# Pooled attention and a gated convolution block: a new order of the tokens in SBUF, 64x64 array tiles, and tanh as the mover

## The chip, the core and the metric

The kernel runs on one core of one Trainium2 chip. TensorE (PE in the profile) multiplies matrices into PSUM, ScalarE (ACT) applies functions element by element, VectorE (DVE) does elementwise arithmetic and copies, GpSimd (POOL) here mainly issues the loads, and SyncE (SP) issues the stores and the copies inside SBUF. Each engine works through its own list of instructions in order. The metric is the device time of one execution in microseconds; the less, the better.

## What is computed

Eight batches, eight heads, 576 tokens, 64 elements a head. Keys and values are averaged over groups of 8 tokens, so each head has 72 pooled keys; the attention output is the input `x` of a feed-forward block with a depthwise convolution over the tokens as its gate.

```python
k_p = k.reshape(B, H, Sp, pool, D).mean(axis=3)      # Sp = 576 / 8 = 72
v_p = v.reshape(B, H, Sp, pool, D).mean(axis=3)
scores = scale * np.matmul(q, k_p.transpose(0, 1, 3, 2))
attn = np.exp(scores - np.max(scores, axis=-1, keepdims=True))
attn = attn / (np.sum(attn, axis=-1, keepdims=True) + 1e-09)
x = np.matmul(attn, v_p)            # then heads side by side: (8, 576, 512)

h = np.maximum(x @ w_in, 0.0)       # (8, 576, 1024)
conv_out = sum over k of conv_w[k] * h shifted by k - 1 tokens
gate = 1.0 / (1.0 + np.exp(-conv_out))
return (h * gate @ w_out)           # (8, 576, 512), float32
```

The inputs are float32; on the chip everything but sums in PSUM and the output is bfloat16.

## The kernel before, in words

**Attention of a batch.** `k_tree` and `v_tree` add up groups of 8 tokens on DVE. `k_turn` transposes the pooled keys on PE and copies them to `kz`; `q_prep` does the same with the queries, 9 transposes at a time, to `qT`. In the queries' load each partition holds 36 neighbouring tokens of one head, and there are 16 such groups (`QG` = 16). So a score tile in PSUM has its columns in the order (two, i, g): token = g * 36 + 2 * i + two. `scores` runs two matmuls of 288 columns a head, and one exp on ACT (line 180) takes the 576 scores of 72 keys from PSUM and writes `attnT`, in the order of the tokens:

```python
out=at.rearrange("s (g i two) -> s two i g", two=2, g=QG),
```

The innermost index that is written is `g`, whose step in `attnT` is 36 elements, 72 bytes. `av` (lines 193 to 204) multiplies a stretch of 128 tokens of `attnT` with the pooled values of 8 heads, and DVE divides by the sums and writes `x`, token by token.

**From x to xT.** The block's first product needs `x` with the 512 features on the partitions. For batch 0, `xt` transposes on PE (20 small transposes) and copies on DVE. For all others `xt_dma` (line 216) does it by a transposing DMA from SBUF to SBUF, five a batch, issued on SP.

**The block.** `mm1(b, fb)` makes one of 8 blocks of 128 hidden features: 8 matmuls of 288 columns, and one relu on ACT into `hT`. `conv(b, g, c2)` works on 4 blocks and 288 tokens: the convolution is a matmul with diagonal weights `dw`, on 32x32 tiles of the array. There are 3 taps x 4 blocks x 4 row tiles = 48 matmuls (line 280), 16 tiles at work together, and for that block `j` puts its row tile `r` into column tile `(r + j) % 4`, so that all but the first block come out rotated by 32 j partitions. Two tanh on ACT (line 289) take them out of PSUM. Since the gate needs `h` in the same rotation, `mm1` issues two DMAs on SP (lines 264, 265) that copy the rotated block within SBUF, for six of 8 blocks, and `load_w_out` loads the rows of `w_out` rotated, in 7 DMAs. `gate` (lines 297, 299) is (tanh + 1) * h on DVE. `mm2` makes one tile of 128 tokens of the output, 8 matmuls of 512 columns, 9 tiles for a pair of batches, copied out by DVE and ACT in turn and stored by SP.

**The order.** It is written out by hand. `start` is batch 0's attention, `first_batch` is batch 0's block with batch 1's attention, and `batch(b)` puts eight `mm1(b)` in a row, with the second half of the convolution of batch b - 1, the steps `att[0]` to `att[6]` of the attention of batch b + 1, the first half of the convolution of b, and 4 or 5 output tiles of earlier batches between them. The keys are pooled and turned one batch earlier (`pool_keys(b + 2)` in the middle, `att[0]` at the end of `batch(b)`). The last batch has no attention beside it. All PSUM tiles come from one pool of four slots (`psum`, two banks each), used in turn, so an instruction on PE that needs a slot waits for the engine that reads the tile of four slots before. The loads of k, q and v have one buffer each; POOL issues the next one when the buffer has been read.

Of the kernel before, what the change touches and what calls it, by code (L numbers as in the profile page):

```python
# [16 lines left out]
def kernel(  # L17
# [10 lines left out]
    nc = tc.nc  # L28
# [7 lines left out]
    QR = S // QG  # L36
    NI = QR // 2
    SC = 288
    NS = S // SC
# [4 lines left out]
    KW = 3  # L44
    QD = 32
    NQ = P // QD
    n_grp = n_fb // NQ
    PAD = 2
    tok0 = [0, 128, 256, 384, S - P]
    row0 = [0, 0, 0, 0, P - S % P]  # L50

# [17 lines left out]
    def slot16(name):  # L69
        return psum.tile([P, 2, 2 * BANK], BF16, name=name, tag="slot")  # L70

    ident = const_pool.tile([P, P], BF16)
    ident32 = const_pool.tile([32, 32], FP32)
    seen = const_pool.tile([1, 1], BF16)
    w_in_sb = const_pool.tile([P, n_dmc, d_ff], BF16)
    w_out_sb = const_pool.tile([P, n_fb, d_model], BF16)
    cw_rows = const_pool.tile([KW * n_fb, P], FP32)
    convw = const_pool.tile([P, KW * n_fb], FP32)
    tile_id = const_pool.tile([P, QD], FP32)
    dw = const_pool.tile([P, KW, n_fb, QD], BF16)  # L80
    kz = [const_pool.tile([P, H, 2, Sp], BF16, name=f"kz{i}") for i in range(2)]
    va = [const_pool.tile([Sp, H, D + 1], BF16, name=f"va{i}") for i in range(2)]
    hT = [
        const_pool.tile([P, n_grp, 2 * NQ - 1, S + 2 * PAD], BF16, name=f"hT{i}") for i in range(2)
    ]

    def h_row(b, fb):
        g, j = divmod(fb, NQ)
        return hT[b % 2][:, g, j + NQ - 1 if j else 0, :]

# [78 lines left out]
    def scores(b, h):  # L169
        ps = slot("sc_ps")  # L170
        for c2 in range(2):
            nc.tensor.matmul(  # L172
                out=ps[0:Sp, c2, 0:SC],
                lhsT=kz[b % 2][:, h, c2, :],
                rhs=st[b]["qT"][:, h].rearrange("d i g -> d (i g)"),
                start=True,
                stop=True,
            )
        at = attnT_pool.tile([Sp, S], BF16, name="attnT")
        nc.scalar.activation(  # L180
            out=at.rearrange("s (g i two) -> s two i g", two=2, g=QG),
            in_=ps[0:Sp, :, 0:SC].rearrange("s two (i g) -> s two i g", g=QG),
            func=ACT.Exp,
            scale=1.0 / (POOL * 8.0),
        )
        st[b].setdefault("at", {})[h] = at
# [24 lines left out]

    def xt_dma(b, i):
        if "xT" not in st[b]:
            st[b]["xT"] = xT_pool.tile([P, n_pairs, S], BF16, name="xT")
        t0, r0 = i * P, row0[i]
        nc.sync.dma_start_transpose(
            out=st[b]["xT"][:, :, t0:t0 + P - r0],
            in_=st[b]["x"][i][r0:P].rearrange("p h d -> p (h d)"),
        )

    def xt(b, tiles):
        if "xT" not in st[b]:
            st[b]["xT"] = xT_pool.tile([P, n_pairs, S], BF16, name="xT")
        ps = slot16("xt_ps")
        w = sum(P - row0[i] for i in tiles)
        y = ps[:, 0, 0:n_pairs * w].rearrange("p (c n) -> p c n", c=n_pairs)
        t = 0
        for i in tiles:
            r0 = row0[i]
            n = P - r0  # L230
            for pr in range(n_pairs):
                nc.tensor.transpose(
                    out=y[:, pr, t:t + n],
                    in_=st[b]["x"][i][r0:P, 2 * pr:2 * pr + 2, :].rearrange("p h d -> p (h d)"),
                    identity=ident[r0:P, r0:P],
                )
            t += n
        t0 = tiles[0] * P
        nc.vector.tensor_copy(out=st[b]["xT"][:, :, t0:t0 + w], in_=y)

    def mm1(b, fb):
        xT = st[b]["xT"]
        ps = slot("h_ps")
        for c in range(NS):
            for dc in range(n_dmc):
                nc.tensor.matmul(  # L246
                    out=ps[:, c, 0:SC],
                    lhsT=w_in_sb[:, dc, fb * P:(fb + 1) * P],
                    rhs=xT[:, dc, c * SC:(c + 1) * SC],
                    start=(dc == 0),  # L250
                    stop=(dc == n_dmc - 1),
                )
        row = h_row(b, fb)
        nc.scalar.activation(  # L254
            out=row[:, PAD:S + PAD].rearrange("p (c n) -> p c n", c=NS),
            in_=ps[:, :, 0:SC],
            func=ACT.Relu,
            scale=0.5,
        )
        g, j = divmod(fb, NQ)  # L260
        if j:
            turned = hT[b % 2][:, g, j, :]
            cut = P - QD * j
            nc.sync.dma_start(out=turned[P - cut:P, PAD:S + PAD], in_=row[0:cut, PAD:S + PAD])
            nc.sync.dma_start(out=turned[0:P - cut, PAD:S + PAD], in_=row[cut:P, PAD:S + PAD])

    def conv(b, g, c2):
# [6 lines left out]
        for kk in range(KW):  # L274
            o0 = PAD - 1 + c2 * SC + kk
            for j in range(NQ):
                row = h_row(b, g * NQ + j)
                for r in range(NQ):
                    c = (r + j) % NQ
                    nc.tensor.matmul(  # L280
                        out=ps[j // 2][QD * c:QD * (c + 1), j % 2, 0:SC],
                        lhsT=dw[QD * r:QD * (r + 1), kk, g * NQ + j, :],
                        rhs=row[QD * r:QD * (r + 1), o0:o0 + SC],
                        start=(kk == 0),
                        stop=(kk == KW - 1),
                    )
        tg = tg_pool.tile([P, NQ, SC], BF16, name="tg")
        for i in range(2):
            nc.scalar.activation(  # L289
                out=tg[:, 2 * i:2 * i + 2, :], in_=ps[i][:, :, 0:SC], func=ACT.Tanh  # L290
            )
        st[b]["tg", g, c2] = tg

    def gate(b, g, c2):
# [6 lines left out]
            in0=t1,  # L301
            in1=hT[b % 2][:, g, 0:NQ, PAD + c2 * SC:PAD + (c2 + 1) * SC],
            op=OP.mult,
# [27 lines left out]

    def load_w_out(j):
        src = moe_w_out.rearrange("(g j p) m -> j p g m", j=NQ, p=P)
        dst = w_out_sb.rearrange("p (g j) m -> j p g m", j=NQ)
        cut = P - QD * j
        nc.gpsimd.dma_start(out=dst[j, P - cut:P], in_=src[j, 0:cut])
        if j:
            nc.gpsimd.dma_start(out=dst[j, 0:P - cut], in_=src[j, cut:P])

    def build_conv_w():  # L340
# [4 lines left out]
        nc.vector.tensor_copy(out=convw, in_=ps[:, 0, 0:KW * n_fb])  # L345
        for r in range(NQ):
            nc.vector.tensor_copy(
                out=tile_id[QD * r:QD * (r + 1), :],
                in_=ident[QD * r:QD * (r + 1), QD * r:QD * (r + 1)],
            )  # L350
        nc.vector.tensor_tensor(
            out=dw.rearrange("p k f j -> p (k f) j"),
            in0=tile_id.unsqueeze(1).to_broadcast([P, KW * n_fb, QD]),
            in1=convw.unsqueeze(2).to_broadcast([P, KW * n_fb, QD]),
            op=OP.mult,
        )

    HH = H // 2

    def start():  # L360
# [7 lines left out]
        for i in range(2):  # L368
            nc.vector.memset(kz[i], 0.0)
            nc.vector.memset(va[i][:, :, D], float(POOL))  # L370
            nc.gpsimd.memset(hT[i][:, :, :, 0:PAD], 0.0)
            nc.gpsimd.memset(hT[i][:, :, :, S + PAD:S + 2 * PAD], 0.0)
        landed(st[0]["k"][0:1, 0, 0, 0:1])
# [16 lines left out]
        landed(st[1]["q"][0:1, 0, 0:1])  # L390
        for j in range(NQ):
            load_w_out(j)
        build_conv_w()
        k_tree(0, 0, HH)
        k_turn(0, 0, HH)
# [17 lines left out]
    def attention(n):  # L413
# [24 lines left out]
        def a5():  # L438
            for i in range(3):
                av(n, i)  # L440
                xt_dma(n, i)

        def a6():
            for i in range(3, 5):
                av(n, i)
                xt_dma(n, i)

        return [a0, a1, a2, a3, a4, a5, a6]

# [8 lines left out]
    def first_batch():  # L458
# [24 lines left out]
        gate(0, 1, 1)  # L483
        pool_keys(2)
        st[2]["att"] = attention(2)
        st[2]["att"][0]()

    def batch(b):
        none = lambda: None
        att = st[b + 1]["att"] if b + 1 < B else [none] * 7  # L490
        tiles = list(range(4)) if b % 2 else list(range(4, 9))

        def tile_out():
            if tiles:
                mm2(b - 1, tiles.pop(0))

        mm1(b, order[0])
        if b > 1:
            conv(b - 1, 1, 0)
        att[1]()  # L500
        if b > 1:
# [3 lines left out]
        if b > 1:  # L505
            conv(b - 1, 1, 1)
        att[2]()
        if b > 1:
# [3 lines left out]
        tile_out()  # L512
        att[3]()

        mm1(b, order[3])
        tile_out()
        att[4]()

        mm1(b, order[4])
        conv(b, 0, 0)  # L520
        att[5]()
        gate(b, 0, 0)
        if b + 2 < B:
            pool_keys(b + 2)
            st[b + 2]["att"] = attention(b + 2)

        mm1(b, order[5])
        conv(b, 0, 1)
        att[6]()
        gate(b, 0, 1)  # L530
# [3 lines left out]
        if len(tiles) > 1:  # L534
            tile_out()

        mm1(b, order[7])
        if b + 2 < B:
            st[b + 2]["att"][0]()
        tile_out()  # L540
# [41 lines left out]
```

## Time and profile before

| what | value |
|---|---|
| median of 3 runs | 363.75 us (363.26 to 364.43) |
| the profiled execution's own time | 364.43 us |
| its span on the core | 362.7 us |
| PE busy | 244.8 us, 67% |
| ACT busy | 244.9 us, 68% |
| DVE busy | 145.7 us, 40% |
| mean granted PE clock | 0.849 |
| read from HBM, written | 32.52 MB, 9.44 MB |

The profile is one execution. "Busy" is time in which an engine had an instruction under way; matmuls overlap each other, so the rate of a stream of matmuls is read from the starts of the groups in the timeline and not from the duration of one. The chain of waits follows the work that ended last back to its cause. A batch in the middle of the run takes 41 us from the first `mm1` of one to that of the next.

### The profile page before, as it was taken

What the parts mean: (1) busy time and instruction counts of PE and PEld (TensorE: products, weight loads), DVE (VectorE), ACT (ScalarE), POOL (GpSimd) and SP (SyncE); (2) the same over time, 40 slices, a digit from 0 to 9 for tenths busy, and PEclk for the clock granted to TensorE, in tenths of its full rate; (3) what the DMA queues carried; (4) which work ended last, traced back from release to release, by engine and by line L of the source; (5) the groups of instructions that cost most, each with busy time, mean ns of one, the idle gap of its engine ahead of it and who ended that gap; (6) DMA issues with size and microseconds to landing.
All of it is one profiled execution on the core that took longest, in us unless ns stands there. A gap on an engine that the chain in (4) does not pass through costs nothing.

```text
span 362.7 us, 7083 instructions
## 1 busy us (share of the span) xinstructions
PE 244.8 (67%) x3013; PEld 148.2 (41%) x3013; DVE 145.7 (40%) x265; ACT 244.9 (68%) x209; POOL 30.3 (8%) x58
## 2 busy tenths in 40 slices
PE   0533874338669486499666966589745985699995
PEld 0413642226235253265334643255423652365642
DVE  5512670095008350084502941075601960072341
ACT  1596289914994179943997369962999389945531
POOL 5525110001000010000100010000100000000000
PEclk9999995557858878969987898969996898579999
DMA  6997994038604954049911986139731531035323
GB/s 110 144 145 118 152 178 75 2 66 143 131 29 73 167 109 101 29 71 198 164 48 57 111 173 125 43 62 187 146 85 41 88 109 47 29 76 153 116 78 145
DMA packets 47155, 37.38 MB, mean 103 GB/s; under 512 B 23036, under 2 KB 41492, under 8 KB 47124
## 3 DMA queue, kind: packets, MB, share of 16 engines
q0 software_dynamic: 16976, 16.27, 30.0%
q1 hardware_dynamic: 30148, 20.67, 23.5%
q8 instruction: 23, 0.38, 0.4%
q14 instruction: 8, 0.07, 0.1%
HBM read 32.52 MB, written 9.44 MB: 116 GB/s over the span
## 4 chain that ended last, share of the span: by engine, by line
ACT 41%; PE 26%; DVE 12%; issue 10%; DMA 9%; POOL 0%; DVEq 0%; SPq 0%; ACTq 0%; POOLq 0%
ACT attnT L180 35%; PE h_ps L246 11%; PE o_ps L312 7%; DMA xT<-x 7%; DVE x L204 3%; PE c_ps L280 3%; PE q_ps L159 3%; ACT tg L289 2%; DMA qr<-in_q_dram 2%; DVE gT L299 2%; PE av_ps L193 2%; ACT hT_107 L254 1%; DVE r L203 1%; ACT hT_108 L254 1%; DVE kdup L135 1%
## 5 line engine op out<-in xcount | busy, mean ns | idle before, releaser
L180 ACT ACTIVATE attnT<-sc_ps 72x576 bf16<-72x576 f32 x64 | 163.2, 2883 | 11.1 <-PE sc_ps L172 11.1
L246 PE MATMUL h_ps<-xT,w_in_sb 128*128 128x288 bf16 x512 | 91.8, 334 | 9.7 <-DMA xT<-x 8.3
L312 PE MATMUL o_ps<-w_out_sb,gT 128*128 128x512 bf16 x288 | 71.0, 396 | 12.4 <-ACT attnT L180 11.5
L246 PEld LDWEIGHTS <-w_in_sb 128*128 128x128 bf16 x512 | 56.0, 112 | 36.3 <-DMA xT<-x 9.5
L203 DVE RECIPROCAL r<-av_ps 128x8 f32<-128x8 f32 x40 | 8.0, 200 | 133.6 <-PE av_ps L193 133.6
L254 ACT ACTIVATE hT_108<-h_ps 128x576 bf16<-128x576 f32 x32 | 23.9, 746 | 42.1 <-PE h_ps L246 42.1
L312 PEld LDWEIGHTS <-gT 128*128 128x128 bf16 x288 | 29.0, 101 | 46.6 <-issue 18.5
L254 ACT ACTIVATE hT_107<-h_ps 128x576 bf16<-128x576 f32 x32 | 24.5, 767 | 33.8 <-PE h_ps L246 33.8
L289 ACT ACTIVATE tg<-c_ps 128x576 bf16<-128x576 f32 x64 | 38.5, 661 | 2.8 <-PE c_ps L280 2.8
L193 PEld LDWEIGHTS <-attnT 72*128 72x128 bf16 x320 | 18.2, 123 | 27.1 <-issue 16.5
L172 PE MATMUL sc_ps<-qT,kz_104 128*72 128x288 bf16 x64 | 14.2, 321 | 22.1 <-ACT attnT L180 21.7
L172 PE MATMUL sc_ps<-qT,kz_103 128*72 128x288 bf16 x64 | 14.4, 341 | 20.6 <-ACT attnT L180 19.4
L204 DVE TENSOR_TENSOR x<-av_ps,r 128x512 bf16<-128x512 f32 x40 | 27.7, 692 | 1.4
L280 PEld LDWEIGHTS <-dw 32*32 32x32 bf16 x1536 | 15.8, 91 | 24.5 <-issue 18.2
L320 ACT COPY o<-o_ps 128x512 f32<-128x512 f32 x16 | 9.4, 589 | 22.4 <-PE o_ps L312 22.4
L322 DVE COPY o<-o_ps 128x512 f32<-128x512 f32 x20 | 13.8, 690 | 25.5 <-PE o_ps L312 25.5
L164 DVE COPY qT<-q_ps 128x1152 bf16<-128x1152 bf16 x16 | 12.1, 758 | 25.6 <-PE q_ps L159 25.4
L193 PE MATMUL av_ps<-va_105,attnT 72*128 72x65 bf16 x160 | 10.5, 232 | 13.7 <-ACT attnT L180 13.5
L172 PEld LDWEIGHTS <-kz_104 128*72 128x72 bf16 x64 | 7.4, 121 | 28.9 <-issue 27.2
L172 PEld LDWEIGHTS <-kz_103 128*72 128x72 bf16 x64 | 8.3, 132 | 26.8 <-issue 22.8
L99 POOL DMA_DIRECT2D kr<-in_k_dram x9 | 7.3, 814 | 136.8 <-DVE t_840 L121 27.2
L280 PE MATMUL c_ps<-hT_107,dw 32*32 32x288 bf16 x768 | 14.3, 340 | 6.2 <-ACT attnT L180 3.8
(162 smaller groups left out, 176.7 us busy)
## 6 DMA issues: line engine op xcount, KB each, us to landing
out_dram<-o SPq DMA_DIRECT2D x36, 256.0 KB, 2.3
qr<-in_q_dram POOLq DMA_DIRECT2D x8, 576.0 KB, 6.1
kr<-in_k_dram POOLq DMA_DIRECT2D x7, 576.0 KB, 8.4
vr<-in_v_dram POOLq DMA_DIRECT2D x7, 576.0 KB, 8.1
hT_107<-hT_107 SPq DMA_DIRECT2D x16, 108.0 KB, 2.2
hT_108<-hT_108 SPq DMA_DIRECT2D x16, 108.0 KB, 2.9
hT_107<-hT_107 SPq DMA_DIRECT2D x16, 72.0 KB, 5.1
hT_108<-hT_108 SPq DMA_DIRECT2D x16, 72.0 KB, 4.5
```

Source lines behind the costliest of these rows:

```text
L164: nc.vector.tensor_copy(out=st[b]["qT"][:, :, i0:i0 + n, :].rearrange("d h i g -> d i h g"), in_=ps[:, 0:n * P].rearrange("d (i h g) -> d ...
L172: nc.tensor.matmul(out=ps[0:Sp, c2, 0:SC], lhsT=kz[b % 2][:, h, c2, :], rhs=st[b]["qT"][:, h].rearrange("d i g -> d (i g)"), start=True, s ...
L180: nc.scalar.activation(out=at.rearrange("s (g i two) -> s two i g", two=2, g=QG), in_=ps[0:Sp, :, 0:SC].rearrange("s two (i g) -> s two i ...
L193: nc.tensor.matmul(out=ps[:, h // 4, c:c + D + 1], lhsT=st[b]["at"][h][:, t0:t0 + P], rhs=va[b % 2][:, h, :], start=True, stop=True,)
L203: nc.vector.reciprocal(out=r, in_=y[:, :, :, D])
L204: nc.vector.tensor_tensor(out=x.rearrange("p (g h) d -> p g h d", g=2), in0=y[:, :, :, 0:D], in1=r.unsqueeze(3).to_broadcast([P, 2, 4, D]) ...
L246: nc.tensor.matmul(out=ps[:, c, 0:SC], lhsT=w_in_sb[:, dc, fb * P:(fb + 1) * P], rhs=xT[:, dc, c * SC:(c + 1) * SC], start=(dc == 0), stop ...
L254: nc.scalar.activation(out=row[:, PAD:S + PAD].rearrange("p (c n) -> p c n", c=NS), in_=ps[:, :, 0:SC], func=ACT.Relu, scale=0.5,)
L280: nc.tensor.matmul(out=ps[j // 2][QD * c:QD * (c + 1), j % 2, 0:SC], lhsT=dw[QD * r:QD * (r + 1), kk, g * NQ + j, :], rhs=row[QD * r:QD * ...
L289: nc.scalar.activation(out=tg[:, 2 * i:2 * i + 2, :], in_=ps[i][:, :, 0:SC], func=ACT.Tanh)
L312: nc.tensor.matmul(out=ps[:, 0, :], lhsT=gT[:, fb, j * P:(j + 1) * P], rhs=w_out_sb[:, fb, :], start=(fb == 0), stop=(fb == n_fb - 1),)
L322: nc.vector.tensor_copy(out=o, in_=ps[:, 0, :])
```

## The change

- exp writes `attnT` in the order (i, two, g): 16 neighbouring elements, then the next 16. The tokens in `attnT`, and in `x`, now stand in the order (i, two, g).
- `xt` serves all batches, `xt_dma` goes. Its transposes take a permutation matrix `perm` (built once by `build_perm`) in place of the identity, write PSUM in runs of 8 elements, and the DVE copy writes `xT` in the order of the tokens, in runs of 16 elements.
- The convolution uses 64x64 tiles: 24 matmuls on 4 tiles. Every second block comes out with its two halves swapped. The tanh of those blocks is split in two of 64 partitions, each of which writes the other half's partitions; so `tg` is in the natural order.
- `hT` has no rotated copies, and their DMAs are gone; `w_out` is loaded in two DMAs.
- The attention has nine steps in place of seven: `a7` and `a8` are the transposes. All nine run within one batch: `att[0]` after the first `mm1`, and so on; `att[7]` ahead of the last `mm1`, `att[8]` after it, ahead of the last output tile.

```diff
     hT = [
-        const_pool.tile([P, n_grp, 2 * NQ - 1, S + 2 * PAD], BF16, name=f"hT{i}") for i in range(2)
+        const_pool.tile([P, n_fb, S + 2 * PAD], BF16, name=f"hT{i}") for i in range(2)
     ]
...
         nc.scalar.activation(
-            out=at.rearrange("s (g i two) -> s two i g", two=2, g=QG),
+            out=at.rearrange("s (i two g) -> s two i g", two=2, g=QG),
             in_=ps[0:Sp, :, 0:SC].rearrange("s two (i g) -> s two i g", g=QG),
...
-    def xt_dma(b, i):
...
     def xt(b, tiles):
...
-        w = sum(P - row0[i] for i in tiles)
-        y = ps[:, 0, 0:n_pairs * w].rearrange("p (c n) -> p c n", c=n_pairs)
...
+        w = len(tiles) * RT
+        y = ps[:, 0, 0:n_pairs * QG * w].rearrange("p (c g r) -> p c g r", c=n_pairs, g=QG)
+        for ii, i in enumerate(tiles):
             for pr in range(n_pairs):
                 nc.tensor.transpose(
-                    out=y[:, pr, t:t + n],
-                    in_=st[b]["x"][i][r0:P, 2 * pr:2 * pr + 2, :].rearrange("p h d -> p (h d)"),
-                    identity=ident[r0:P, r0:P],
+                    out=y[:, pr, :, ii * RT:(ii + 1) * RT],
+                    in_=st[b]["x"][i][:, 2 * pr:2 * pr + 2, :].rearrange("p h d -> p (h d)"),
+                    identity=perm,
                 )
...
+        nc.vector.tensor_copy(
+            out=st[b]["xT"].rearrange("p c (g r) -> p c g r", g=QG)[:, :, :, r0:r0 + w - skip],
+            in_=y[:, :, :, skip:w],
+        )
...
-        g, j = divmod(fb, NQ)
-        if j:
-            turned = hT[b % 2][:, g, j, :]
-            cut = P - QD * j
-            nc.sync.dma_start(out=turned[P - cut:P, PAD:S + PAD], in_=row[0:cut, PAD:S + PAD])
-            nc.sync.dma_start(out=turned[0:P - cut, PAD:S + PAD], in_=row[cut:P, PAD:S + PAD])
...
-            for j in range(NQ):
-                row = h_row(b, g * NQ + j)
-                for r in range(NQ):
-                    c = (r + j) % NQ
...
+            for p2 in range(2):
+                for j in range(2):
+                    fb = g * NQ + 2 * p2 + j
+                    for r in range(2):
+                        c = (r + j) % 2
+                        nc.tensor.matmul(
+                            out=ps[j][HP * c:HP * (c + 1), p2, 0:SC],
+                            lhsT=dw[HP * r:HP * (r + 1), kk, fb, :],
+                            rhs=hT[b % 2][HP * r:HP * (r + 1), fb, o0:o0 + SC],
+                            start=(kk == 0),
+                            stop=(kk == KW - 1),
+                        )
         tg = tg_pool.tile([P, NQ, SC], BF16, name="tg")
-        for i in range(2):
+        pairs = tg.rearrange("p (p2 j) n -> p p2 j n", j=2)
+        nc.scalar.activation(out=pairs[:, :, 0, :], in_=ps[0][:, :, 0:SC], func=ACT.Tanh)
+        for c in range(2):
+            r = 1 - c
             nc.scalar.activation(
-                out=tg[:, 2 * i:2 * i + 2, :], in_=ps[i][:, :, 0:SC], func=ACT.Tanh
+                out=pairs[HP * r:HP * (r + 1), :, 1, :],
+                in_=ps[1][HP * c:HP * (c + 1), :, 0:SC],
+                func=ACT.Tanh,
             )
...
-            out=dw.rearrange("p k f j -> p (k f) j"),
-            in0=tile_id.unsqueeze(1).to_broadcast([P, KW * n_fb, QD]),
...
+            in0=tile_id.unsqueeze(1).to_broadcast([P, KW * n_fb, HP]),
...
+    def build_perm():
+        nc.vector.tensor_copy(
+            out=perm.rearrange("p (g r) -> p r g", r=RT),
+            in_=ident.rearrange("p (r g) -> p r g", r=RT),
         )
...
-        for j in range(NQ):
-            load_w_out(j)
+        for i in range(2):
+            load_w_out(i)
         build_conv_w()
+        build_perm()
...
     def attention(n):
...
+        def a7():
+            xt(n, [0, 1])
+
+        def a8():
+            xt(n, [2, 3])
+            xt(n, [4])
...
         mm1(b, order[4])
         conv(b, 0, 0)
-        att[5]()
+        att[4]()
+        pool_keys(b + 2)
         gate(b, 0, 0)
-        if b + 2 < B:
-            pool_keys(b + 2)
-            st[b + 2]["att"] = attention(b + 2)

         mm1(b, order[5])
         conv(b, 0, 1)
-        att[6]()
+        att[5]()
         gate(b, 0, 1)

         mm1(b, order[6])
         tile_out()
         if len(tiles) > 1:
             tile_out()
-
+        att[6]()
+
+        att[7]()
         mm1(b, order[7])
-        if b + 2 < B:
-            st[b + 2]["att"][0]()
+        att[8]()
         tile_out()
```

## The prediction, written before the changed kernel ran

> **What bounds the kernel now.** First the page's chain of work and its costliest groups: the engine that is longest on the chain has one line that stands out.
>
> ```profile
> ACT 41%; PE 26%; DVE 12%; issue 10%; DMA 9%; POOL 0%; DVEq 0%; SPq 0%; ACTq 0%; POOLq 0%
> L180 ACT ACTIVATE attnT<-sc_ps 72x576 bf16<-72x576 f32 x64 | 163.2, 2883 | 11.1 <-PE sc_ps L172 11.1
> L289 ACT ACTIVATE tg<-c_ps 128x576 bf16<-128x576 f32 x64 | 38.5, 661 | 2.8 <-PE c_ps L280 2.8
> ```
>
> Exp and tanh read the same 576 float32 from PSUM and write 576 bfloat16, yet one exp is 2.88 us and one tanh 0.66. They differ in the function and in the place of the written elements (72 bytes apart against side by side). Second, the rates, from ACT's timeline, of instructions that follow each other:
>
> ```profile
> 13.13 20.06 ACT L180 ACTIVATE attnT<-sc_ps 72x576 bf16<-72x576 f32 x8 [11.11 <-PE sc_ps L172]
> 348.50 2.28 ACT L289 ACTIVATE tg<-c_ps 128x576 bf16<-128x576 f32 x4
> ```
>
> 2.51 us for each exp, 0.57 for each tanh. Third, who waits for it:
>
> ```profile
> PE sc_ps L172 <- ACT attnT L180: 41.1, 30, 2.1
> PE av_ps L193 <- ACT attnT L180: 22.2, 12, 2.2
> PE o_ps L312 <- ACT attnT L180: 11.5, 9, 1.5
> PE h_ps L246 <- DMA xT<-x: 8.3, 4, 4.7
> PE c_ps L280 <- ACT attnT L180: 7.4, 6, 1.6
> ```
>
> PE stands 82 us for exp (slots of `psum`, or `attnT` itself) and 8 for the transposing DMA. Last, the stages (length, PE, PEld, DVE, ACT, POOL busy, granted clock, DMA share, GB/s): start, batch 0, a middle batch, the last batch, the tail.
>
> ```profile
> 0.00:39.06 39.06, 13.06 (x103) 9.54 (x104) 16.86 (x41) 21.34 (x9) 16.70 (x40) 1.00 0.91 134
> 39.06:82.66 43.60, 23.61 (x356) 16.31 (x356) 19.36 (x34) 29.38 (x24) 3.26 (x4) 0.69 0.49 87
> 211.10:252.60 41.50, 30.07 (x378) 18.14 (x379) 17.78 (x31) 30.39 (x26) 2.22 (x3) 0.88 0.57 105
> 329.88:347.80 17.92, 17.92 (x290) 10.70 (x289) 6.96 (x11) 10.19 (x17) 0.00 (x0) 1.00 0.45 146
> 347.80:362.70 14.90, 10.37 (x137) 4.68 (x136) 4.39 (x7) 4.03 (x7) 0.00 (x0) 1.00 0.29 107
> ```
>
> The last batch, which has no attention beside it, takes 17.9 us with PE never idle at full clock; the same block with attention takes 41.5. So the middle batches are set by exp, and below it lies a PE bound that these rows allow to be added up.
>
> **The parts of the change.**
>
> *Exp in runs of 16.* Bounds: 0.57 us each, as tanh, or 2.51, as now. Nearest is DVE's `qT` copy, whose output too stands in runs of 16 (1152 elements in 0.76 us, 0.66 ns each; the plain `xT` copy takes 0.68 for 1024, the same rate): runs of 16 cost nothing there. I take 0.6. The Trainium skill (SBUF — State Buffer, the note on cachelines) says an engine needs at least two hits in a 16-byte line for full bandwidth; this run has eight, the present order one. ACT in a middle batch: 8 exp at 0.6, 8 relu at 0.65, 4 x 3 tanh at 0.57, 2.25 copies at 0.58: 18.1 us in place of 30.4. The third tanh costs 32 x 0.57 = 18 us of ACT in all, hidden under PE while ACT's sum is below PE's; only the tail's last pair shows.
>
> *Transposes on PE.* Seven batches x 20. The row is `q_prep`, 9 in 0.50 us where they follow each other:
>
> ```profile
> 288.48 0.50 PE q_ps L159 x9
> ```
>
> So 20 x 0.056 = 1.1 us a batch. The new output has steps in PSUM, which no row shows for PE: at worst the 0.31 us of a lone transpose in the groups (`xt_ps`, 309 ns), 6.2 us a batch; no gain is possible. I take 1.1, the nearest in kind and density. The Trainium skill (TensorE: Matmul & The Clock Gate, on PE-mode transposes) speaks against moving them: it gives about 275 ns each inside a kernel. By that figure it would be 5.5 us a batch and the forecast some 30 us later; the row says 56 ns. DVE gains three copies (0.68, 0.68, 0.28) a batch, 17.8 to 19.4 us: still under PE. The wait for the DMA (5 to 8 us on the chain at each batch's first `mm1`) goes; late next is the copy of tile 4, under the last output tile's 1.73 us.
>
> *The convolution.* Now 48 matmuls in 0.67 us, three rounds of 16 tiles; then six rounds of four. A round can't be shorter than a stream of 288 columns (`mm1`: eight in 0.98, 0.122 each): 0.73. As long as now's rounds (0.22): 1.34. So +0.06 to +0.67 a call; I take +0.2, nearer the stream, since a round has four weights to load and not 16. 32 calls: 6 us (2 to 21).
>
> *Copies of h.* 96 DMA issues leave SP's queue, 35 transposes too; SP keeps 36 stores. The chain has 1.9 us of waiting for these copies at one place: no more is counted. `w_out`: two DMAs for seven on POOL, same bytes; its wait for landings sets the time, not the issue: nothing. `perm` and a `dw` twice as wide put about 1.2 us (0.96 again, and a copy of 0.25) ahead of `k_tree(0)` on DVE; q lands at 9.45, after the turned keys (8.9): 0.3 us shows.
>
> *PE's sum for a middle batch.* 17.92 (8 `mm1`, 4 conv, 4 output tiles) + 0.87 (half a tile, the mean is 4.5) + scores 16 x 0.122 = 2.0 + `q_prep` 1.0 + `k_turn` 0.3 + `av` 40 x 0.055 = 2.2 (16 took 0.78 to 0.87 at the densest) + 1.1 transposes + 0.8 conv = 26.2. Above ACT (18.1) and DVE (19.4), so PE is the bound. Not all will be packed: each convolution wants two of four slots, which three tanh (1.7 us) hold longer than two did, and at step `att[4]` ACT gets tanh x 3, exp x 2, relu, tanh x 3 in a row, some 5.5 us against PE's 3; following the slots by hand there, PE waits 0.8 to 1.5 us. With DVE's order (`pool_keys`, 2.6 us, now ahead of `gate` and the `x` of `av`) I allow 2.2 a batch: 28.4, against 41.2 (247.2 us from 82.66 to 329.88, six batches).
>
> *The start.* Eight exp at 0.6 save 15.3 us; `av` then waits for v_tree, whose v lands at 15.7 and which is through by 18.5; `mm1` 5.8 us later as now: 24.5. `w_in` is complete at 23.6. So 14.5 off. *Batch 0*: v of batch 1 is issued at 29.74 and takes 8.1 us: 37.8, behind landings which the change doesn't move. Then on DVE: v_tree 2.3, gates 3 x 1.2, five `x` at 0.88, three copies 1.7: 49.8. I take 51 for batch 1's first `mm1` (82.66 now).
>
> *Sum.* 51 + 6 x 28.4 + last batch 17.9 + 0.8 + tail 14.9 + 1.0 (a tanh, two conv) = 256 us of span. Outside it 364.43 - 362.70 = 1.7, and the profiled run is 0.7 above the median: **257 us**.
>
> **Rivals.** (a) *Exp stays as slow*: its time is in the function, or 16-element runs don't help. For: no ACT row has such runs. Against: the `qT` copy. ACT's batch is then 8 x 2.51 + 5.2 + 6.8 + 1.3 = 33.4, and of its 11 idle us some 6 stay: 39.4; start 38.5, batch 0 43: 38.5 + 43 + 6 x 39.4 + 18.7 + 15.9 + 1 = about 353. (b) *A PE part is dear*: transposes at 0.31 (+5 a batch, 7 batches: 292), or the four tiles take turns (24 x 0.122 = 2.93 a call, +2.26 x 32: with the 6 taken out, 323). Against: 16 tiles work together now at 0.22 a round. (c) *The loads become the bound*: the queues' shares, 30.0% and 23.5% of 362.7, are 194 us of 16 engines, 24 a batch with the copies that go; under 28.4, so it is hidden; it decides from 28.4 up, and a tenth above that, 31 a batch, is 273. (d) *Slower*: PE's clock. It drops to 0.5 after idle stretches (0.69 in batch 0, where one `mm1` took 2.08 in place of 0.98). If a packed PE were held at half, a batch would be 52 us and the whole over 450; it decides from a clock of 26.2 / 41.2 = 0.64 down. Against: the last batch ran at 1.00.
>
> **How the numbers follow.** My case 80% (242 to 283: conv at +0.06 and stalls of 0.5 a batch give 242, conv at +0.67 and stalls of 4 give 283; its own range, 245 to 272, is between); (b) and (c), or an exp between the ends, 13% (272 to 323); (a) 4%; (d) 3%. The range 243 to 288 takes in nearly all of the first and the cheaper part of (b) and (c), and leaves out (a), (d) and the dear ends of (b). 0.3% is about what a measurement here can tell from no change: faster 0.96, same 0.01, slower 0.03.
>
> **What would show it.** Right: exp near 0.6 us a piece; no PE wait for `attnT` above a us; the middle batches at 27 to 30 us with PE over 90% busy and the clock near 1; conv at 0.73 to 1.0 a call; `mm1` starting at 24 to 26 us. Wrong: exp above 1.2; `xt_ps` at 0.2 us a piece in its stream; PE waiting for tanh or for slots over 4 us a batch; the first `mm1` of a batch waiting for DVE's `xT`.

## The result, and the profile after

The changed kernel takes 258.87 us (median of 4 runs, 257.91 to 259.77) against 363.5 us for the one before beside it (361.25 to 364.43): a ratio of 0.713, 95% interval 0.709 to 0.717. The forecast was 257, with a range of 243 to 288. The profiled execution has a span of 257.0 us.

The same views in the same order as before. First the page: the chain by engine, the exp group and the group of the two half tanh.

```profile
PE 57%; ACT 20%; DVE 12%; DMA 6%; issue 3%; POOL 0%; POOLq 0%
L176 ACT ACTIVATE attnT<-sc_ps 72x576 bf16<-72x576 f32 x64 | 37.0, 646 | 18.5 <-PE sc_ps L168 18.3
L273 ACT ACTIVATE tg<-c_ps 64x576 bf16<-64x576 f32 x64 | 41.3, 645 | 1.2
```

Exp was 2883 ns a piece and is 646, the same as the half tanh (645); the 163.2 us of the group became 37.0. PE now leads the chain. ACT's timeline gives the pace of instructions that follow each other (start, length, count):

```profile
124.39 0.65 ACT L270 ACTIVATE tg<-c_ps 128x576 bf16<-128x576 f32 x1
125.06 1.30 ACT L273 ACTIVATE tg<-c_ps 64x576 bf16<-64x576 f32 x2
126.39 1.18 ACT L176 ACTIVATE attnT<-sc_ps 72x576 bf16<-72x576 f32 x2
```

0.59 us for each exp (0.6 was assumed, 2.51 before) and 0.65 for each half tanh. Third, from the list of what PE waits for, the rows that the argument needs: us in total, times, the longest.

```profile
PE kT_ps L143 <- DVE kdup L131: 5.1, 3, 4.3
PE xt_ps L216 <- DVE x L200: 3.1, 6, 0.9
PE h_ps L233 <- DVE xT L223: 2.5, 2, 2.2
PE c_ps L261 <- ACT attnT L176: 2.2, 6, 0.4
PE c_ps L261 <- ACT tg L273: 1.1, 6, 0.2
```

The 82 us of waiting for exp are now 2.2 us. Last the stages (length, then PE, PEld, DVE, ACT, POOL busy, granted clock, DMA share, GB/s): start, batch 0, batch 1, a middle batch with four output tiles and one with five, the last batch, the tail.

```profile
0.00:24.86 24.86, 11.61 (x103) 8.70 (x104) 17.72 (x40) 5.80 (x9) 10.54 (x30) 0.92 0.90 128
24.86:52.91 28.05, 21.09 (x262) 14.97 (x262) 17.43 (x32) 16.98 (x28) 6.34 (x9) 0.93 1.00 152
52.91:81.01 28.10, 26.28 (x246) 17.60 (x246) 18.87 (x32) 13.75 (x23) 3.04 (x4) 0.90 0.65 114
...
109.72:137.03 27.31, 26.00 (x295) 17.58 (x294) 19.47 (x34) 17.63 (x29) 2.22 (x3) 1.00 0.54 104
137.03:165.75 28.72, 27.64 (x304) 18.38 (x303) 18.87 (x33) 18.81 (x31) 2.22 (x3) 1.00 0.54 109
...
221.93:240.89 18.96, 18.74 (x197) 11.50 (x198) 6.77 (x11) 13.34 (x21) 0.00 (x0) 1.00 0.13 50
240.89:257.00 16.11, 10.57 (x89) 5.03 (x88) 4.42 (x7) 5.64 (x9) 0.00 (x0) 0.98 0.28 106
```

In a middle batch PE is busy for 95 or 96% of the time at clock 1.00, where it was 72% at 0.88. Of the 105.7 us that went from the span, 14.2 went in the start (39.06 to 24.86), 15.6 in batch 0 (43.6 to 28.05), 78 in the six batches (247.2 to 169.0); the last batch and the tail gave back 1.0 and 1.2.

### The profile page after: what moved, and what is told of

It is laid out like the page before. It is cut to its first block, busy times and chain, and to the rows that moved or that the text cites. A ratio compares the mean times of both kernels' runs of the same rounds, so it can differ in the third digit from the quotient of the medians.

```text
span 257.0 us, 5560 instructions
## 1 busy us (share of the span) xinstructions
PE 223.3 (87%) x2385; PEld 148.2 (58%) x2385; DVE 158.2 (62%) x285; ACT 147.2 (57%) x241; POOL 28.0 (11%) x53
## 4 chain that ended last, share of the span: by engine, by line
PE 57%; ACT 20%; DVE 12%; DMA 6%; issue 3%; POOL 0%; POOLq 0%
PE o_ps L298 24%; PE h_ps L233 18%; ACT attnT L176 6%; PE c_ps L261 6%; DMA qr<-in_q_dram 6%; ACT tg L273 5%; PE q_ps L155 4%; DVE x L200 4%; ACT tg L270 3%; DVE o L308 3%; ACT hT_108 L240 3%; ACT hT_109 L240 2%; PE xt_ps L216 2%; PE sc_ps L168 1%; PE av_ps L189 1%
## 5 line engine op out<-in xcount | busy, mean ns | idle before, releaser
L233 PE MATMUL h_ps<-xT,w_in_sb 128*128 128x288 bf16 x512 | 75.7, 294 | 5.9 <-DVE xT L223 2.5
L176 ACT ACTIVATE attnT<-sc_ps 72x576 bf16<-72x576 f32 x64 | 37.0, 646 | 18.5 <-PE sc_ps L168 18.3
L273 ACT ACTIVATE tg<-c_ps 64x576 bf16<-64x576 f32 x64 | 41.3, 645 | 1.2
L240 ACT ACTIVATE hT_109<-h_ps 128x576 bf16<-128x576 f32 x32 | 20.8, 651 | 33.2 <-PE h_ps L233 32.9
L240 ACT ACTIVATE hT_108<-h_ps 128x576 bf16<-128x576 f32 x32 | 20.9, 652 | 19.6 <-PE h_ps L233 19.3
L261 PEld LDWEIGHTS <-dw 64*64 64x64 bf16 x768 | 22.1, 105 | 13.9 <-issue 12.0
L306 ACT COPY o<-o_ps 128x512 f32<-128x512 f32 x16 | 9.4, 586 | 28.2 <-PE o_ps L298 28.2
L270 ACT ACTIVATE tg<-c_ps 128x576 bf16<-128x576 f32 x32 | 20.8, 650 | 3.4 <-PE c_ps L261 3.3
L261 PE MATMUL c_ps<-hT_108,dw 64*64 64x288 bf16 x384 | 16.7, 287 | 2.6 <-ACT attnT L176 1.1
L216 PE MATMUL xt_ps<-perm,x 128*128 128x128 bf16 x160 | 14.0, 227 | 4.8 <-DVE x L200 3.1
L261 PE MATMUL c_ps<-hT_109,dw 64*64 64x288 bf16 x384 | 16.4, 286 | 1.6 <-ACT attnT L176 1.1
L216 PEld LDWEIGHTS <-x 128*128 128x128 bf16 x160 | 10.8, 100 | 7.2 <-DVE x L200 5.9
L155 PE MATMUL q_ps<-ident,qr 128*128 128x128 bf16 x144 | 12.0, 237 | 1.9 <-DMA qr<-in_q_dram 1.9
```

What stands on the lines that cost most here:

```text
L155: nc.tensor.transpose(out=ps[:, i * P:(i + 1) * P], in_=st[b]["q"][:, i0 + i, :], identity=ident)
L176: nc.scalar.activation(out=at.rearrange("s (i two g) -> s two i g", two=2, g=QG), in_=ps[0:Sp, :, 0:SC].rearrange("s two (i g) -> s two i ...
L216: nc.tensor.transpose(out=y[:, pr, :, ii * RT:(ii + 1) * RT], in_=st[b]["x"][i][:, 2 * pr:2 * pr + 2, :].rearrange("p h d -> p (h d)"), id ...
L233: nc.tensor.matmul(out=ps[:, c, 0:SC], lhsT=w_in_sb[:, dc, fb * P:(fb + 1) * P], rhs=xT[:, dc, c * SC:(c + 1) * SC], start=(dc == 0), stop ...
L240: nc.scalar.activation(out=hT[b % 2][:, fb, PAD:S + PAD].rearrange("p (c n) -> p c n", c=NS), in_=ps[:, :, 0:SC], func=ACT.Relu, scale=0.5,)
L261: nc.tensor.matmul(out=ps[j][HP * c:HP * (c + 1), p2, 0:SC], lhsT=dw[HP * r:HP * (r + 1), kk, fb, :], rhs=hT[b % 2][HP * r:HP * (r + 1), f ...
```

## The experiments

Theory: exp's write, 72 bytes from element to element, was the bound; with it gone PE is, and the other parts are judged by what they add to PE or make it wait for. The main rival: the gain comes from the DMAs that the change removes.

### Exp alone, in the kernel before

```diff
-            out=at.rearrange("s (g i two) -> s two i g", two=2, g=QG),
+            out=at.rearrange("s (i two g) -> s two i g", two=2, g=QG),
```

> The kernel before with one line changed: exp writes (i, two, g). Nothing puts the tokens back in order, so the convolution sees other neighbours and the output is not the reference's; every instruction and transfer is otherwise the one of before. Theory (the whole gain is exp's write, and the other parts of the change are its price): ACT's batch falls to 30.4 - 8 x 1.92 = 15 us, PE's sum is 17.92 + 0.87 + 2.0 + 1.0 + 0.3 + 2.2 = 24.3 a batch, plus 1 to 3 us of waiting for the transposing DMA: 26.5 a batch, 24.9 + 28 + 6 x 26.5 + 17.9 + 14.9 + 1.7 = about 246, between 240 and 262. Rival (the DMAs that the change removed would have become the bound): the first mm1 of each batch waits 5 us and more for xT, 31 a batch, 270 to 285.

Measured: 266.31 us (263.81 to 268.89), ratio 0.729 (0.720 to 0.737). The one line brings 27.1% of the time, of 28.7% for the whole change. It landed between the two sums, closer to the rival's 270. PE's waits and one batch of this kernel show why.

```profile
PE h_ps L246 <- DMA xT<-x: 15.7, 6, 4.7
PE kT_ps L147 <- DVE kdup L135: 12.2, 3, 8.3
```

```profile
120.71:149.92 29.21, 25.27 (x368) 16.18 (x371) 17.00 (x30) 15.12 (x26) 2.21 (x3) 0.94 0.82 158
```

PE's 25.3 us is 1.0 above the sum of 24.3. The DMA wait is 2.6 us at each of six places, as allowed. The sum missed two things. Batch 1's first `mm1` starts at 57.95 us and not at 52.9, behind one wait of 8.3 us for the keys of batch 2; the kernel before has 6.0 us of this wait at the same place. And a middle batch takes 28.5 us in the mean, not 26.5: beside the wait itself, in this batch the matmuls behind it run at half the pace for a while (eight of `mm1` in 2.05 us, where they take 1.07 otherwise), at a mean clock of 0.94. So exp is the cause of the gain, and the transposing DMA is late once the batch is short.

### The old exp in the changed kernel

```diff
-            out=at.rearrange("s (i two g) -> s two i g", two=2, g=QG),
+            out=at.rearrange("s (g i two) -> s two i g", two=2, g=QG),
```

> The changed kernel with exp writing in steps of 72 bytes again, as before; the tokens then stand in another order than the permutation expects, so the output is not the reference's, with the same instructions. Theory (exp's write is the cause): exp is back at 2.5 us, ACT bounds the middle batches at 33.4 + 6 = 39 us, about 353. Rival (the gain came from the DMAs that went): 260 to 300.

Measured: 386.08 us (385.33 to 386.91), ratio 1.060 (1.051 to 1.068): slower than the kernel before, though 131 fewer DMAs are issued inside SBUF (96 copies of h, 35 transposes). The rival falls. The price of 353 was wrong too. Two middle batches and PE's waits:

```profile
171.30:214.50 43.20, 32.03 (x292) 20.35 (x294) 19.46 (x34) 33.06 (x29) 2.22 (x3) 0.80 0.34 66
214.50:259.72 45.22, 34.81 (x300) 21.52 (x302) 18.86 (x33) 34.26 (x31) 2.23 (x3) 0.77 0.34 69
```

```profile
PE sc_ps L168 <- ACT attnT L176: 36.5, 26, 2.1
PE c_ps L261 <- ACT attnT L176: 26.0, 18, 2.2
```

ACT is busy for 33.1 and 34.3 us a batch, as summed (33.4). But it idles for 10 to 11 us, as before, and not for 6. The DMA wait was not what had kept ACT idle. Around the change of batch at 214.50 no exp is ready: the last one ends near 203.5 us, and the next starts at 223.09, behind scores that PE begins at 222.65, after `av`, the transposes, output tiles, `mm1` and convolutions. And the convolution's wait for slots that exp holds grew from 7.4 to 26.0 us.

### The convolution part undone

```diff
-            for p2 in range(2):
-                for j in range(2):
...
+            for j in range(NQ):
+                row = h_row(b, g * NQ + j)
+                for r in range(NQ):
...
+            nc.sync.dma_start(out=turned[P - cut:P, PAD:S + PAD], in_=row[0:cut, PAD:S + PAD])
+            nc.sync.dma_start(out=turned[0:P - cut, PAD:S + PAD], in_=row[cut:P, PAD:S + PAD])
```

> The changed kernel with the convolution part undone: 48 matmuls on 32x32 tiles, two tanh, rotated copies of h by DMA, w_out rotated. Theory (the 64x64 tiles are a loss on PE, now that PE is the bound): a call is 0.67 us again where it is 0.86 to 1.11, some 0.25 x 32 = 8 us less: 249 to 253. Rival (the rotated copies of h come too late now that a batch is 28 us, or the third tanh was hidden and the copies are not): PE waits 1 to 2 us a batch for hT, 262 to 270.

Measured: 250.29 us (248.75 to 251.77), ratio 0.687 (0.680 to 0.694), which is 8.6 us below the changed kernel. The theory's sum is met, and this part of the change is a loss of 2.6% of the time before. How the loss divides is another matter: the theory put all of it on the length of the calls, and the run with two tanh, below, divides it otherwise. The middle batch with four tiles:

```profile
109.42:135.29 25.87, 24.53 (x388) 16.52 (x390) 19.26 (x34) 14.37 (x25) 2.21 (x3) 1.00 0.72 145
```

25.9 us against 27.3. The 96 copies of h are back and take the DMA share from 0.54 to 0.72; PE's list of waits names none of them.

From this kernel too comes the clean price of the new transposes (PE's timeline, nothing waited between the two rows): eight start within 0.45 us, 56 ns each, though they write PSUM in runs of 8 elements.

```profile
131.01 0.61 PE L221 MATMUL xt_ps<-perm,x 128*128 128x128 bf16 x8
131.46 1.14 PE L238 MATMUL h_ps<-xT,w_in_sb 128*128 128x288 bf16 x8
```

That is the 0.056 of the forecast. The 275 ns that the Trainium skill (TensorE: Matmul & The Clock Gate, PE-mode transpose) gives for one inside a kernel is nearer to the length of one here (227 ns in the changed kernel's costliest groups) than to the pace of a stream.

### The transposing DMA in the changed kernel

```diff
         def a5():
-            av(n, 0)
-            av(n, 1)
+            for i in range(2):
+                av(n, i)
+                xt_dma(n, i)
...
         def a7():
-            xt(n, [0, 1])
+            pass
```

> The changed kernel with x transposed by DMA again in batches 1 to 7, issued right after each av; the tokens stay in the order (i, two, g), so the output is not the reference's. PE loses 20 transposes (1.2 us) and DVE three copies a batch. Theory: after the last av PE has 2.7 us of work left in the batch and a transposing DMA takes 3 to 8, so each batch's first mm1 waits 3 to 5 us: 271. Rival (the DMA is hidden, and the transposes on PE were a loss): 250.

Measured: 268.64 to 278.05 us in four runs. They scatter too widely for a ratio with an interval, so only the direction is taken: each is above the changed kernel's highest, 259.77. In the profiled run PE waits for `xT` in nearly all batches:

```profile
PE h_ps L244 <- DMA xT<-x: 26.1, 13, 9.5
```

That is 3.7 us a batch over seven batches, where 3 to 5 were expected. This is the slowest of the four runs and one wait of it is 9.5 us, so the size is rough. The rival (hidden, 250) falls, since the shortest run is 268.64.

### The third tanh

```diff
-        for c in range(2):
-            r = 1 - c
-            nc.scalar.activation(
-                out=pairs[HP * r:HP * (r + 1), :, 1, :],
-                in_=ps[1][HP * c:HP * (c + 1), :, 0:SC],
-                func=ACT.Tanh,
-            )
+        nc.scalar.activation(out=pairs[:, :, 1, :], in_=ps[1][:, :, 0:SC], func=ACT.Tanh)
```

> The changed kernel with one tanh in place of the two halves, so two a convolution, as before; the swapped halves are not moved back, so the output is not the reference's. It measures what the third tanh costs. Theory (hidden, since PE is the bound): 0.6 in the tail, 0.5 in batch 0 and up to 0.5 a batch of the waits of the second convolution: 1 to 4 us less, 255 to 258. Rival (PE runs at ACT's pace around the convolutions): 32 x 0.6 = 19 us less, 240.

Measured: 250.84 us (249.75 to 252.35), ratio 0.693 (0.687 to 0.699): 8.0 us less by the medians, 7 by the ratios. Neither sum fits: the third tanh is mostly hidden, but it costs about twice the most that "hidden" was given. On ACT, too, it is dearer than taken. Three tanh hold ACT for 2.00 us (from 124.39 to the exp at 126.39, in the rows of the result above), and in the kernel with two they hold it for 1.08 (121.56 to 122.64). That is 0.92 for the third, and not 0.57, or 29 us in all, of which 7 to 8 show in the time. PE's timeline of the changed kernel shows the place, the second convolution of a batch's first half, behind `att[4]`:

```profile
123.42 0.94 PE L261 MATMUL c_ps<-hT_109,dw 64*64 64x288 bf16 x24
124.29 0.68 PE L168 MATMUL sc_ps<-qT,kz_104 128*72 128x288 bf16 x4
125.09 1.14 PE L233 MATMUL h_ps<-xT,w_in_sb 128*128 128x288 bf16 x8
126.41 0.31 PE L261 MATMUL c_ps<-hT_109,dw 64*64 64x288 bf16 x2 [0.19 <-ACT tg L273]
127.09 0.93 PE L261 MATMUL c_ps<-hT_109,dw 64*64 64x288 bf16 x22 [0.36 <-ACT attnT L176]
127.94 0.69 PE L189 MATMUL av_ps<-va_106,attnT 72*128 72x65 bf16 x16
```

The first call is 0.87 us from start to next start; the second takes from 126.16 (the first `mm1` group's pace, 1.07, after 125.09) to 127.94, 1.78: it waits for one slot that tanh still reads and for another that exp still reads. With two tanh the same call is unbroken:

```profile
123.33 0.93 PE L261 MATMUL c_ps<-hT,dw 64*64 64x288 bf16 x24
124.20 0.69 PE L189 MATMUL av_ps<-va,attnT 72*128 72x65 bf16 x16
```

Its batch is 26.2 us (107.14 to 133.33) in place of 27.3. So of the convolution part's loss the third tanh is 7 to 8 us; the longer calls, 0.87 for 0.67, are 0.2 x 32 = 6.4. Together that is more than the 8.6 that undoing the part brought, so the undone kernel loses something elsewhere. 2.9 us of that lie ahead of batch 1, whose first `mm1` starts at 54.28 us there and at 51.33 with two tanh alone: DVE waits 3.0 us for a rotated copy. From there on the undone kernel gains 3.7 us over the one with two tanh, where 28 shorter calls alone would make 5.6. What takes the other 2 us stays open.

### Batch 0's gates put off, and the order of the loads

In the undone kernel batch 1's first `mm1` starts at 54.3 us, later than the changed kernel's 52.9. In `first_batch`:

```diff
         att[5]()
-        gate(0, 1, 0)
         conv(0, 1, 1)
         att[6]()
-        gate(0, 1, 1)
         att[7]()
```

> The changed kernel with the convolution part undone (32x32 tiles, two tanh, rotated copies of h), and the two gates of batch 0's second half put off to batch 1, as all later batches have them. With the convolution undone, batch 1's first mm1 starts at 54.3 us: DVE waits 3 us for a rotated copy of h ahead of the x of tiles 2 to 4, and does two gates (1.2 each) ahead of xT. Theory (that chain on DVE sets the start of batch 1): mm1 at 49 to 50 us, 4 to 5 us less in all, 245 to 247. Rival (the keys of batch 2 arrive no earlier, and PE waits for them instead): 249 to 251.

Measured: 247.57 us (246.44 to 247.71), ratio 0.683 (0.677 to 0.689). `mm1` starts at 49.8, as expected, but at most 2.7 of the 4 to 5 us stay, and by the ratios, whose intervals overlap (0.687 before this change), 1.5. The rival's wait took the place of the other: PE stands 2.95 us for the keys of batch 2. DVE's timeline, and POOL's issue of that load:

```profile
52.12 1.22 DVE L122 TENSOR_TENSOR t<-kr 72x2048 bf16<-72x2048 bf16 x1 [2.36 <-DMA kr<-in_k_dram]
```

```profile
38.70 0.86 POOL L100 DMA_DIRECT2D kr<-in_k_dram  x1 [1.40 <-DMA vr<-in_v_dram]
```

The keys of batch 2 were issued at 38.7 us behind seven loads of `w_out`, and landed at 52.1. The last run moves those loads behind `pool_keys(1)`:

```diff
         pool_keys(1)
+        landed(st[1]["q"][0:1, 0, 0:1])
+        for j in range(NQ):
+            load_w_out(j)
```

> The kernel with the convolution part undone and batch 0's gates put off, and in addition POOL issues the load of the keys of batch 2 ahead of the seven loads of w_out, not after them. There the keys landed at 52.1 us and PE waited 3 us for them at 51.9, in a stretch in which the DMA engines were busy without a break. Theory (order of loads): the keys are issued at 31 in place of 38.7 and land by 45, the wait goes, w_out lands by 52, before the first output tile at 60: 2 to 3 us less, 244.5 to 246. Rival (the DMA engines are full until 52 us whatever the order, and what is put back, q and v of batch 2 or w_out, is then the late one): 247 to 249.

Measured: 246.57 us (245.96 to 246.99), ratio 0.676 (0.671 to 0.680). The interval overlaps that of the run before, so a gain is not shown. The wait for the keys is gone (the sums of keys start at 49.23, right behind `xT`), and the queries are late by 1.2 us instead:

```profile
53.79 1.14 PE L160 MATMUL q_ps<-ident,qr 128*128 128x128 bf16 x9 [1.19 <-DMA qr<-in_q_dram]
```

The DMA share from 24 to 52 us is 0.98 here, and in both orders one load came late. That fits the rival: the loads set the pace up to 52 us whatever their order. Two orders are not enough to show it. Both of these kernels are faster than the kernel before and than the changed kernel (0.683 and 0.676 against 0.713).

### How exp's time depends on what it writes

```diff
+        run = (4, 4, 4, 2, 2, 2, 1, 1)[h]
...
-            out=at.rearrange("s (i two g) -> s two i g", two=2, g=QG),
+            out=at.rearrange("s (m two r) -> s two m r", two=2, r=run),
```

> The changed kernel with exp writing shorter runs: heads 0 to 2 in runs of 4 elements (8 bytes, every 16), heads 3 to 5 in runs of 2 (4 bytes, every 8), heads 6 and 7 in single elements 4 bytes apart. The tokens stand in other orders, so the output is not the reference's; only the pace of exp in each group is of interest (now 0.59 us in runs of 16, 2.51 for single elements 72 bytes apart). Theory 1 (each new run costs the same, 1.9 us / 576 = 3.3 ns): 144 runs 1.1 us, 288 runs 1.5, 576 runs 2.5. Theory 2 (what counts is how many elements of the pass fall into one 16-byte line, two being enough, as the Trainium skill, SBUF — State Buffer, has it; here each pass puts four into every line): 0.6 us in all three groups.

ACT's timeline of one batch: three exp in runs of 4, three in runs of 2, two in single elements.

```profile
119.87 1.72 ACT L177 ACTIVATE at_run<-sc_ps 72x576 bf16<-72x576 f32 x3 [1.02 <-PE sc_ps L168]
123.76 1.72 ACT L177 ACTIVATE at_run<-sc_ps 72x576 bf16<-72x576 f32 x3
127.95 1.47 ACT L177 ACTIVATE at_run<-sc_ps 72x576 bf16<-72x576 f32 x2
```

Three in runs of 16 also took 1.72 us in the changed kernel. So runs of 4 and 2 cost nothing; single elements 4 bytes apart cost 0.73 each where runs of 16 cost 0.59 (2 in 1.47 against 2 in 1.18). A price for each run falls (it gave 1.1, 1.5 and 2.5). Theory 2 holds for two of three groups and misses the third by 0.14. Single elements stand in both the 0.73 and the 2.51, so what made 2.51 of it is the distance between them, 72 bytes in place of 4. At which distance between these two the price rises was not tried.

## Why the prediction was right, point by point

**The bound.** Exp's write, shown by the swap in both directions: in the old kernel it brings 27.1% of the time, and the changed kernel without it is 6% slower than before.

**Exp in runs of 16.** 0.6 was taken, 0.59 measured. DVE's `qT` copy was a fair stand-in for ACT.

**Transposes on PE.** 56 ns each, as taken; the trace's row was right and the dearer end, 0.31, not reached. In exchange the transposing DMA's wait went, which with exp alone made fast was 15.7 us at six places, 2.6 each. The forecast's 5 to 8 us at each batch's first `mm1` was a misreading: these are the lengths of transfers on the chain, in four batches, and PE's wait for them was 8.3 us in all. No term of the sum rests on it, since the sum is made of PE's work. With exp out of the way the wait is worth more than those 8.3 us: the undone-convolution kernel, 250.3, and exp alone, 266.3, differ in the transposes and the order of the attention's steps, 16 us.

**The convolution.** +0.2 a call was taken, 0.87 less 0.67 measured. As a choice it was a loss, as the plus in that sum said, and the third tanh made it a larger one.

**The third tanh.** Here a statement failed: "hidden under PE while ACT's sum is below PE's; only the tail's last pair shows". It shows with 7 to 8 us, since PE waits not for ACT's sum but for one slot at one place. Its price on ACT was also too low, 0.57 taken and 0.92 measured. The stall that the forecast allowed, 2.2 us a batch, included that very place (0.8 to 1.5 there) and so held the cost under another name. In the middle batch 0.9 goes at that convolution, 0.2 at an earlier one (1.11 us for 0.87), and 0.5 at the transposes; the last 0.5 is there with two tanh too.

**The stages.** Start 24.5 against 24.86; batch 1 from 51 against 52.91; six batches of 28.4 against 28.2; last batch 18.7 against 18.96; tail 15.9 against 16.1. The sum is off by 1.9 us up to batch 1 and by 1.4 the other way in the six batches, so no large errors cancel between the stages. Inside a batch there was some luck. The scores took 2.6 us (0.95, 0.84 and 0.80) where 2.0 was taken, and `av` 1.7 (0.76 and 0.95) where 2.2 was: over six batches some 3.5 us too low and 3 too high. Batch 0 took 28.05 us, 1.5 more than the 26.5 of the forecast. At its end PE waits 2.15 us for DVE's `xT`, which follows the gates; with two tanh batch 0 takes 27.0 (24.34 to 51.33), so 1 us of the excess comes with the third tanh.

**The rivals.** (a), priced at 353, would have been 386: it had supposed that ACT's idle time would shrink by 5 us a batch with the DMA wait, and it did not. That also moves it to the other side, slower than before, where the forecast had named only the clock. (c) may have a grain of truth in the start and in batch 0, where the DMA share is 0.90 and 1.00; in the middle batches, at 0.54, the loads are hidden, as was said. (b) and (d) are not seen: four tiles do work together (0.145 us a round, where one stream of 288 columns takes 0.122), and the clock is 1.00 in the packed batches.

## What to carry to other kernels

Compare instructions that do the same amount of work: one function at 2.9 us beside another at 0.66 on the same shape is a question about its access pattern, and a change of layout that other steps can absorb may be worth more than any reordering. When the bound is removed, what was hidden has to be priced again in the shorter batch: a DMA for which PE had waited 8 us in all cost it 16 us of waiting once exp alone was fast. "Hidden because the engine's sum is lower" isn't enough where the engine holds a buffer that the bound engine needs next; follow the slots.

## What the runs showed of the hardware

- ACT writing bfloat16, 576 elements of 72 partitions: 0.57 to 0.59 us in runs of 16, 4 and 2 (three in 1.72 for each of them), 0.73 in single elements 4 bytes apart, 2.51 in single elements 72 bytes apart. The Trainium skill (SBUF — State Buffer, the note on cachelines) asks for at least two hits in a 16-byte line. The two ends agree with it; the 0.73 of a pattern with four hits a line is above what it says.
- ACT can write other partitions than it reads: tanh from the first 64 of PSUM to the last 64 of `tg` at 0.65 us, as long as a whole tanh in place (0.65). Half the partitions is no cheaper. Two such halves in a row take 0.65 each (1.30), whole tanh in a row 0.57 (four in 2.28); whether that comes of the other partitions or of reading one PSUM tile twice was not tried.
- Six rounds of four 64x64 tiles take 0.87 us (0.145 a round of 288 columns), three rounds of sixteen 32x32 tiles 0.67 (0.22 a round). Four times fewer tiles do not make the call four times, or even twice, as long.
